# Row layout of the k and q loads, 64x64 transposes, and new orders at the start and the end of a block-sparse attention + soft MoE kernel

## The chip, the core and the metric

The kernel runs on one core of a Trainium2 chip. The metric is the device time of one execution in microseconds (us). Five engines work side by side, each through its own instructions in order: TensorE (PE in the profile, PEld for its weight loads), VectorE (DVE), ScalarE (ACT), GpSimd (POOL) and SyncE (SP, which here only issues DMAs). Matmul results land in PSUM, everything else on the chip lives in SBUF; both have 128 partitions.

## The reference

Four batches (B) of eight heads (H), 768 positions (S), head size 64 (D). In each head the keys are cut into 24 chunks of 32 positions. Of each chunk the minimum and the maximum of k give an upper bound of the score for each query; the six chunks with the highest bound (among the causal ones) are kept, and a causal softmax attention runs over them:

```python
ub = sum(max(q * k_min, q * k_max), axis=-1)         # [q, 24], -1e9 where not causal
top_chunks = argsort(ub)[..., -6:]
scores = where(chunk in top_chunks and causal, q @ k.T / 8, -1e9)
x = softmax(scores) @ v                               # [3072, 512] over all heads
logits = x @ phi                                      # [3072, 32]: 8 experts x 4 slots
d = softmax(logits, axis=0);  slot_input = d.T @ x
slot_out[e] = relu(slot_input[e] @ w1[e]) @ w2[e]
out = softmax(logits, axis=1) @ slot_out
```

## The kernel before, in words

**Pairs.** Work goes in 16 pairs of heads, four pairs to a batch, the two heads of a pair on partitions 0-63 and 64-127. Per pair i:

- `load` (L163) brings k and q from HBM by a POOL-issued DMA, cast to bf16 on the way, two pairs to a DMA from pair 2 on. Partition p holds, of each head, the six rows 6p to 6p+5: for a pair two pieces of 384 numbers. Pair 0 goes another way: two SP DMAs in f32 (L184), then `cast` (L589) to bf16, one head on DVE (L591) and one on ACT (L592).
- `transposes` (L232) makes kT and qT: 12 matmuls (L240), six row groups g times two heads h. Each takes 128 partitions x 64 columns as weights against the 128-column identity and writes 64 partitions x 128 columns: `ps[h*64:(h+1)*64, g, :]`. All of a pair's k (or q) lies in one PSUM tile. `evac_T` (L246, L250) copies it to SBUF, on ACT, and puts the columns into the order of the positions.
- `kmin`, `kmax` (L259, L265, DVE), `heads` (L271, bd), `qneg`, `qpos` (L279, L289; qpos of pair 0 on ACT, L287) prepare the bound; `ubound` (L292) is its matmuls (L299, L309); `select` (L315) takes the eight largest of each row (L320) and makes a mask (L322 on POOL, L323 on DVE), which `ns_transposes` (L331) and `evac_ns` (L339) turn.
- `scores` (L342): per group of blocks, matmuls of q and k (L349) and of the mask (L359), each pair of them on the two halves of the partitions. `expo` (L373, ACT) is the exponential, `mask` (L383, POOL) the causal cut, `pv` (L397) the product with v, `normalise` (L409, L410), `x_transposes` (L419), `evac_x` (L430).

Two PSUM tiles hold scores (pool `p_sc`), two hold everything that is transposed or small (`p_tp`), one holds the products with v (`p_at`).

**MoE.** After each batch: logits (L442), a running maximum, exponentials, `moe_dispatch` (L529; L537 the slot inputs, L541 `zt`, the sums). Weights w1, w2 come by POOL DMAs (L150, L160) spread over the whole kernel; all POOL DMAs run in one queue, one after another.

**Order.** Nothing reorders instructions: each engine does them as the program issues them. A head written out by hand (L594 to L670) does pairs 0 and 1 up to their selections, all scores of pair 0 and the preparation of pair 2; `warm` (L227) issues matmuls whose results nobody reads. From pair 1 on, strings (PLAIN, LOGITS, SLOTS, AFTER, BEFORE_LAST, FINAL; L731 to L736) give the order, and `step` and `final` carry out their words: sc, ex, mk, pv for scores, expo, mask and pv; trk, trq, evk, evq for transposes and their copies of pair i+2; ub, sel, ns, evns for the bound of pair i+1. In FINAL, `pl`, `nl`, `xl`, `el`/`ela` are pv, normalise, transposes and copies (DVE/ACT) of the last pair, three spans of rows each; `lgt` and `lgl` the logits of the last batch without and with the last pair's columns; `pma` the maximum over the first five row blocks of them, joined at L866 with the sixth; `cs` 18 small matmuls (L821) that sum the combine weights of the first three batches, `inv` their reciprocal (L813).

**Tail.** After FINAL: the softmax of the last batch's logits (L866 to L902), `moe_dispatch` of the last batch, two expert layers (L934, L975, L1001, L1011) and the output, by halves of the columns and then whole (L1045, L1031, L1034, L1075), written by SP.

Of the kernel before, what the change touches and what calls it, by code (L numbers as in the profile page):

```python
# [9 lines left out]
F32 = mybir.dt.float32  # L10
# [6 lines left out]
NEG = -1e9  # L17
# [42 lines left out]
def kernel(  # L60
# [75 lines left out]
    for nm in ("k", "q"):  # L136
        ring[nm] = [inp.tile([P, 4, NQT * D], BF16, name=f"{nm}_in{x}") for x in range(2)]
    for x, nm in enumerate(("k", "q")):
        spare = w_sb[EARLY - 4][:, x * 4 * NQT * D:(x + 1) * 4 * NQT * D]
        ring[nm].append(spare.rearrange("p (h c) -> p h c", h=4))  # L140
# [21 lines left out]

    def load(i, nm, n=1):  # L163

        b, j = divmod(i, NPB)
        t = ring[nm][i // 2 % 3][:, 2 * (i % 2):2 * (i % 2 + n)]
        src = {"k": k, "q": q}[nm][b, 2 * j:2 * (j + n)]
        nc.gpsimd.dma_start(out=t, in_=src.rearrange("h (p g) d -> p h (g d)", p=P))
        for x in range(n):
            st[nm, i + x] = t[:, 2 * x:2 * x + 2]  # L170
# [11 lines left out]
    stage = [w_sb[x].bitcast(F32).rearrange("p (h c) -> p h c", c=512)[:, :2, :NQT * D] for x in range(EARLY - 2, EARLY)]  # L182
    for t, src in zip(stage, (k, q)):
        nc.sync.dma_start(out=t, in_=src[0, :2].rearrange("h (p g) d -> p h (g d)", p=P))  # L184
# [47 lines left out]
    def transposes(i, nm, runs=((0, NQT),), home=(p_tp, "tp")):  # L232

        src = st.pop((nm, i))
        st[nm + "ps", i] = []
        for g0, g1 in runs:
            ps = home[0].tile([P, g1 - g0, P], BF16, name="tr_ps", tag=home[1])
            for g in range(g0, g1):
                for h in range(2):
                    nc.tensor.matmul(  # L240
                        ps[h * 64:(h + 1) * 64, g - g0, :], lhsT=src[:, h, g * D:(g + 1) * D], rhs=ident,
                        is_transpose=True,
                    )
            st[nm + "ps", i].append((g0, g1, ps))

    def evac_T(i, nm, *copies):  # L246

        t = tp3.tile([P, S], BF16, name=nm + "T", tag=nm + "T")
        for (g0, g1, ps), copy in zip(st.pop((nm + "ps", i)), copies or (nc.scalar.copy,)):
            copy(  # L250
                t.rearrange("d (p g) -> d p g", g=NQT)[:, :, g0:g1],
                ps.rearrange("d g p -> d p g"),
            )
        st[nm + "T", i] = t
# [334 lines left out]
    def cast(n, nm):  # L589
        st[nm, 0] = ring[nm][0][:, :2]  # L590
        nc.vector.tensor_copy(st[nm, 0][:, 0], stage[n][:, 0])  # L591
# [15 lines left out]
    qneg(0)
    qpos(0)
    nc.vector.tensor_tensor(schunk[:, :, :, 0], squad[:, :, 0, :], squad[:, :, 1, :], op=ALU.add)
    spread_mask(0, NJ, nc.gpsimd.tensor_copy)  # L610
    warm(10)
    ubound(0)
    spread_mask(NJ, NQT, nc.scalar.copy)
    select(0)
    transposes(1, "k", ((0, NQT),), (p_sc, "sc"))
    evac_T(1, "k")
    transposes(1, "q", ((0, NQT),), (p_sc, "sc"))
    evac_T(1, "q")
    load_v(1)
    load(4, "q", 2)  # L620
    warm(3)
    ns_transposes(0)
    evac_ns(0)
    kmin(1)
    kmax(1)
    heads(1)
    qneg(1)
    qpos(1)
    for g in range(5):
        scores(0, g)  # L630
        expo(0, g, g < 4)
        if g == 1:
            load(6, "k", 2)
            warm(3)
        if g == 2:
            warm(1)
    load(6, "q", 2)
    ubound(1)
    select(1)
    load_v(2)  # L640
    load_w(1)
    mask(0, 4)
    transposes(2, "k")
    evac_T(2, "k")
    nc.gpsimd.dma_start(out=phi_sb, in_=moe_phi.rearrange("(hg p) s -> p hg s", p=P))
    scores(0, 5)
    warm(3)
    expo(0, 5)
# [18 lines left out]
    nc.vector.memset(pm_pad, 0.0)
# [68 lines left out]
    FINAL = """sc:1 sc:0 norm sc:2 ex:1 pv:0 pv:2 pv:3 pv:4 mk:1 ctc pv:5 pv:1 ex:0 ex:2 sc:3 xt mk:0 ex:3 norm1 sc:4 mk:2 ex:4 xt1 mk:3 evx pl:0 evx1 sc:5 mk:4 pl:2 pl:1 nl:0 pl:3 nl:1 xl:0 pl:4 lgt el:0 mz lh:2 ex:5 pl:5 lh:3 xl:1 cs nl:2 lgl:0 xl:2 ela:1 lgl:1 ela:2 pma lgl:2 inv"""  # L736
# [40 lines left out]
    def final(what):  # L777
# [20 lines left out]
        elif name == "lgt":  # L798
            st["lgt"] = p_at.tile([P, 2, 512], F32, name="lgt_ps", tag="at")
            st["lg12"] = st["lgt"][:, 0, :2 * NQT * NS].rearrange("p (t o s) -> p t o s", t=NQT, o=2)  # L800
            moe_logits(BL, range(NDG - 1), st["lg12"])
        elif name == "lgl":
            moe_logits(BL, range(NDG - 1, NDG), st["lg12"], range(*SPANS[n]))
        elif name == "pma":
            nc.vector.tensor_reduce(
                pm_a, st["lg12"][:, :NQT - 1, 0, :].rearrange("p t s -> p s t"), axis=AX.X, op=ALU.max)
# [18 lines left out]
    pm_a = small.tile([P, NS], F32, name="pm_a", tag="pm_a")  # L825
# [39 lines left out]
    pm = small.tile([P, NS], F32, name="pm", tag="pm")  # L865
    nc.vector.tensor_tensor(pm, pm_a, lg1[:, NQT - 1], op=ALU.max)  # L866
# [152 lines left out]
    relu(0)  # L1019
    experts_in(1, 0)  # L1020
# [93 lines left out]
```

## Time and profile before

| | |
|---|---|
| median of 3 runs | 157.98 us (157.34 to 158.03) |
| the profiled execution | 157.53 us, of which the span from first to last instruction is 155.8 us |
| granted TensorE clock, mean | 0.987 |

| engine | busy in the span |
|---|---|
| PE | 138.0 us, 89% |
| DVE | 122.4 us, 79% |
| ACT | 122.4 us, 79% |
| POOL | 95.3 us, 61% |

A line of the timeline or of the groups reads: start, duration (both us), engine, line of the kernel, operation, tile written <- tiles read, shape; xN puts N instructions together, and the duration is then from the first start to the last end. In brackets stands how long the engine sat idle before it and what ended that.

### The profile page before, as it was taken

How to read it: one execution, taken by the hardware profiler on the slowest of the kernel's cores; microseconds unless marked ns; L12 is line 12 of the kernel's file. 1: busy time of each engine (PE TensorE's matmuls, PEld its weight loads, DVE VectorE, ACT ScalarE, POOL GpSimd, SP SyncE). 2: the span in 40 equal slices, each digit the busy share in tenths (PEclk: the TensorE clock that was granted, in tenths of full speed). 3: DMA queues.
4: the chain of work that ended last, by engine and by line, in shares of the span. 5: the costliest groups of instructions: out<-in, count | busy, mean ns of one | idle time of the engine just before them, and what ended most of it. 6: DMA issues, size and time to landing. Idle time of an engine off the chain costs nothing.

```text
span 155.8 us, 6087 instructions
## 1 busy us (share of the span) xinstructions
PE 138.0 (89%) x2515; PEld 90.9 (58%) x2515; DVE 122.4 (79%) x450; ACT 122.4 (79%) x167; POOL 95.3 (61%) x196
## 2 busy tenths in 40 slices
PE   7998979999999999999999999999989899776700
PEld 2443546767667676757766776766758745553200
DVE  4777889889898999999999999999775660459800
ACT  3678899999999899999989999998887333437700
POOL 6966992984878769476946947496593990000000
PEclk9999999999999999999999999999999999999995
DMA  4999999999999999999999999999999999989996
GB/s 149 211 183 215 195 196 196 214 178 197 211 217 188 195 214 184 197 207 219 192 196 203 203 207 196 199 194 215 204 210 210 209 195 198 133 271 346 375 403 230
DMA packets 46171, 33.31 MB, mean 214 GB/s; under 512 B 26304, under 2 KB 41664, under 8 KB 46144
## 3 DMA queue, kind: packets, MB, share of 16 engines
q0 software_dynamic: 41328, 25.86, 114.1%
q1 hardware_dynamic: 4816, 7.08, 12.8%
q8 instruction: 19, 0.31, 0.7%
q14 instruction: 8, 0.07, 0.1%
HBM read 52.49 MB, written 6.29 MB: 377 GB/s over the span
## 4 chain that ended last, share of the span: by engine, by line
PE 47%; DVE 23%; ACT 12%; issue 5%; POOL 4%; DMA 2%; DVEq 0%; SPq 0%; ACTq 0%; POOLq 0%
PE sc_ps L349 9%; PE at_ps L397 9%; ACT e_sb L373 8%; PE sc_ps L359 6%; PE tr_ps L240 4%; PE xT_ps L419 3%; DVE mx L320 3%; DMA w_sb<-in_q_dram 2%; PE h_ps L934 2%; DVE mm L259 2%; DVE mm L265 2%; PE ub_ps L299 2%; ACT o_sb L1031 2%; POOL e_sb L383 2%; DVE o_sb L1034 2%
## 5 line engine op out<-in xcount | busy, mean ns | idle before, releaser
L373 ACT ACTIVATE e_sb<-sc_ps 128x768 bf16<-128x768 f32 (+2 forms) x96 | 83.1, 927 | 5.5 <-PE sc_ps L359 4.6
L383 POOL TENSOR_SCALAR_AFFINE_SELECT e_sb<-e_sb 128x256 bf16<-128x256 bf16 x96 | 37.7, 413 | 21.2 <-ACT e_sb L373 20.8
L349 PE MATMUL sc_ps<-qT,kT 64*128 64x384 bf16 (+3 forms) x260 | 37.7, 306 | 1.4 <-ACT e_sb L373 1.3
L359 PE MATMUL sc_ps<-nsT,smask 64*128 64x384 bf16 (+2 forms) x296 | 37.6, 284 | 0.1
L397 PE MATMUL at_ps<-v_t,e_sb 128*128 128x65 bf16 x630 | 26.3, 193 | 0.2
L397 PEld LDWEIGHTS <-e_sb 128*128 128x128 bf16 x630 | 22.4, 97 | 5.2 <-issue 2.8
L320 DVE MAX8 mx<-ub_ps 128x8 f32<-128x8 f32 (+1 forms) x192 | 16.8, 163 | 5.6 <-PE ub_ps L309 3.6
L349 PEld LDWEIGHTS <-kT 64*128 64x128 bf16 x260 | 13.0, 93 | 8.4 <-issue 2.2
L174 POOL DMA_DIRECT2D v_t<-in_v_dram x16 | 16.6, 1041 | 0.5 <-PE sc_ps L359 0.5
L359 PEld LDWEIGHTS <-smask 64*128 64x128 bf16 x296 | 14.8, 95 | 3.5 <-issue 0.6
L410 DVE TENSOR_TENSOR x_sb<-at_ps,inv 128x768 bf16<-128x768 f32 (+3 forms) x18 | 15.6, 868 | 0.6
L259 DVE TENSOR_REDUCE mm<-kT 128x24 bf16<-128x768 bf16 x16 | 15.1, 943 | 0.1
L265 DVE TENSOR_REDUCE mm<-kT 128x24 bf16<-128x768 bf16 x16 | 15.1, 943 | 0.0
L250 ACT COPY qT<-tr_ps 128x768 bf16<-128x768 bf16 x16 | 13.1, 816 | 1.4 <-PE tr_ps L240 1.4
L250 ACT COPY kT<-tr_ps 128x768 bf16<-128x768 bf16 (+1 forms) x16 | 12.7, 796 | 0.1
L230 PE MATMUL warm_ps<-ones_sq 128*128 128x512 bf16 x29 | 9.2, 451 | 1.1 <-DVE ones_sq L180 1.1
L150 POOL DMA_DIRECT2D w_sb<-in_moe_w_dram x14 | 10.0, 715 | 0.0
L299 PEld LDWEIGHTS <-qpn 128*128 128x128 bf16 x192 | 6.0, 96 | 6.2 <-issue 3.6
L430 DVE COPY xT_sb<-xT_ps 128x768 bf16<-128x768 bf16 (+1 forms) x16 | 8.6, 536 | 1.2 <-PE xT_ps L419 1.2
L299 PE MATMUL ub_ps<-bd,qpn 128*128 128x48 bf16 x192 | 7.8, 184 | 1.0 <-DVE qpn L279 0.9
L419 PE MATMUL xT_ps<-ident,x_sb 128*128 128x128 bf16 x96 | 8.4, 220 | 0.0
L323 DVE TENSOR_TENSOR ns_t<-ub_ps,mx 128x288 bf16<-128x288 f32 x16 | 7.3, 457 | 0.5
(170 smaller groups left out, 220.5 us busy)
## 6 DMA issues: line engine op xcount, KB each, us to landing
w_sb<-in_moe_w_dram POOLq DMA_DIRECT2D x14, 1024.0 KB, 16.8
out_dram<-o_sb SPq DMA_DIRECT2D x14, 256.0 KB, 2.9
v_t<-in_v_dram POOLq DMA_DIRECT2D x16, 192.0 KB, 13.8
out_dram<-o_sb SPq DMA_DIRECT2D x5, 512.0 KB, 4.5
w_half<-in_moe_w_dram POOLq DMA_DIRECT2D x8, 256.0 KB, 9.5
k_in<-in_k_dram POOLq DMA_DIRECT2D x5, 384.0 KB, 11.2
q_in<-in_q_dram POOLq DMA_DIRECT2D x5, 384.0 KB, 11.9
w_sb<-in_k_dram POOLq DMA_DIRECT2D x2, 384.0 KB, 10.8
```

Of the source, the lines that this page charges most:

```text
L174: nc.gpsimd.dma_start(out=v_t[i % NV][:, :, :, :D], in_=v[b, 2 * j:2 * j + 2].rearrange("h (g p) d -> p h g d", p=P),)
L250: copy(t.rearrange("d (p g) -> d p g", g=NQT)[:, :, g0:g1], ps.rearrange("d g p -> d p g"),)
L259: nc.vector.tensor_reduce(mm[:, 0, 0, :], kT, axis=AX.X, op=ALU.min)
L265: nc.vector.tensor_reduce(mm[:, 1, 0, :], kT, axis=AX.X, op=ALU.max)
L299: nc.tensor.matmul(o, lhsT=qpn[:, x, t * P:(t + 1) * P], rhs=bd[:, x], start=(t == 0 and x == 0), stop=False,)
L320: nc.vector.max(mx[:, a, :], ub[:, a, :max(8, 4 * t + 4)])
L349: nc.tensor.matmul(ps[:, h, c:c + w], lhsT=kT[r, kg * P:(kg + 1) * P], rhs=qT[r, qs], start=True, stop=False,)
L359: nc.tensor.matmul(ps[:, h, c + (f - t0) * P:c + (l - t0) * P], lhsT=smask[r, x, kg].rearrange("p a b -> p (a b)"), rhs=nsT[r, (f - x * NJ ...
L373: nc.scalar.activation(e[:, :, :w], st.pop(("scps", i, g))[:, :, :w], func=ACT.Exp, scale=scale)
L383: nc.gpsimd.affine_select(out=e[:, :, c:c + P], in_=e[:, :, c:c + P], compare_op=ALU.is_ge, fill=0.0, base=0, pattern=[[0, 2], [1, P]], ch ...
L397: nc.tensor.matmul(o, lhsT=st["e", i, g][:, h, c:c + P], rhs=v_t[i % NV][:, h, kg, :D + 1], start=(kg == 0), stop=(kg == t),)
L410: nc.vector.tensor_tensor(st["x", b][:, t0:t1, 2 * j:2 * j + 2, :].rearrange("p t h d -> p h t d"), at[:, :, :, :D], inv.broadcast_to([P, ...
```

## The change

Three parts.

1. **Layout and transposes.** Partition p now holds 12 consecutive rows of one head (partitions 0-63 the first head of the pair, 64-127 the second): one piece of 768 numbers instead of two of 384. A transpose takes a quarter of the array: 64 partitions x 64 columns of weights against a 64-column identity, to 64 partitions x 64 columns. There are 24 of them for one k or q instead of 12, in the order g, then h. The casts of pair 0 are split by columns (row groups 0-5 and 6-11), no longer by head.
2. **Head.** The hand-written lines become a string HEAD and `head()`, with another order: among others, on ACT the copy of kT comes before the cast of q; on DVE `qneg` of pair 0 comes before `bd`; the transposes of pair 1 stand partly before the bound of pair 0; the bound of pair 1 (ub:1) stands after the fourth group of scores, not after the fifth; `sc:5` and the q transposes of pair 2 come earlier and `ex:5` later; two memsets (pm_pad, pm_lo) move from pair 2's preparation to the start; the first weight load is issued after `spreadp`.
3. **End.** The logits of the last batch without the last pair's columns are cut in two (`lgt:0`, `lgt:1`) and come after the last products with v (`pl:5`); `cs` comes after the last logits; the last copy of xT goes from ACT to DVE; one maximum over all six row blocks replaces the two steps; the reciprocal of the sums comes after the first `relu`; in the last dispatch `zt` comes before the slot inputs.

The orders PLAIN to BEFORE_LAST, and so the work of pairs 1 to 14 but for the transposes' form, are unchanged.

```diff
-        ring[nm] = [inp.tile([P, 4, NQT * D], BF16, name=f"{nm}_in{x}") for x in range(2)]
+        ring[nm] = [inp.tile([P, 2, S], BF16, name=f"{nm}_in{x}") for x in range(2)]
...
+    def head_pairs(t, b, j, n):
+        src = t[b, 2 * j]
+        return bass.AP(src.tensor, src.offset, [[S, P], [P * S, n], [1, S]])
+
     def load(i, nm, n=1):
         b, j = divmod(i, NPB)
-        t = ring[nm][i // 2 % 3][:, 2 * (i % 2):2 * (i % 2 + n)]
-        src = {"k": k, "q": q}[nm][b, 2 * j:2 * (j + n)]
-        nc.gpsimd.dma_start(out=t, in_=src.rearrange("h (p g) d -> p h (g d)", p=P))
+        t = ring[nm][i // 2 % 3][:, i % 2:i % 2 + n]
+        nc.gpsimd.dma_start(out=t, in_=head_pairs({"k": k, "q": q}[nm], b, j, n))
...
-        nc.sync.dma_start(out=t, in_=src[0, :2].rearrange("h (p g) d -> p h (g d)", p=P))
+        nc.sync.dma_start(out=t, in_=head_pairs(src, 0, 0, 1))
...
+    nc.vector.memset(pm_pad, 0.0)
+    nc.vector.memset(pm_lo, 0.0)
...
-    def transposes(i, nm, runs=((0, NQT),), home=(p_tp, "tp")):
+    NG, HP = 12, 64
+    def transposes(i, nm, runs=((0, NG),), home=(p_tp, "tp")):
...
-            ps = home[0].tile([P, g1 - g0, P], BF16, name="tr_ps", tag=home[1])
+            ps = home[0].tile([P, g1 - g0, HP], BF16, name="tr_ps", tag=home[1])
             for g in range(g0, g1):
                 for h in range(2):
+                    r = slice(h * HP, (h + 1) * HP)
                     nc.tensor.matmul(
-                        ps[h * 64:(h + 1) * 64, g - g0, :], lhsT=src[:, h, g * D:(g + 1) * D], rhs=ident,
-                        is_transpose=True,
+                        ps[r, g - g0, :], lhsT=src[r, g * D:(g + 1) * D], rhs=ident[r, r], is_transpose=True,
                     )
...
-    def cast(n, nm):
-        st[nm, 0] = ring[nm][0][:, :2]
-        nc.vector.tensor_copy(st[nm, 0][:, 0], stage[n][:, 0])
-        nc.scalar.copy(st[nm, 0][:, 1], stage[n][:, 1])
+    def cast(n, nm, h, copy):
+        st[nm, 0] = ring[nm][0][:, 0]
+        c = slice(h * S // 2, (h + 1) * S // 2)
+        copy(st[nm, 0][:, c], stage[n][:, 0, c])
...
+    HEAD = """w:6 w:1 ka kd lv:0 caus qd qgrp trk:0 w:1 evk:0 qa trq:0 kmin:0 w:4 kmax:0 w:1 evq:0 lk:4 qsn:0 bd:0 squad schunk w:1 trk:1:s qsp:0 ub:0 w:1 spreada w:2 spreadp lw evk:1 w:1 sel:0 w:1 trq:1:s evq:1 ns:0 evns:0 sc:0 kmin:1 lv:1 kmax:1 lq:4 sc:1 lk:6 w:2 w:1 qsp:1 qsn:1 ex:0 sc:2 mk:0 w:1 ex:1 sc:3 ex:2 mk:2 bd:1 trk:2 ub:1 ex:3 mk:1 sel:1 sc:4 sc:5 evk:2 lq:6 kmin:2 mk:3 ex:4 trq:2 w:1 mk:4 once lv:2 ns:1 w:1 evns:1 w:1 evq:2 lw w:1 kmax:2 phi identf bd:2 qsn:2 ex:5 qsp:2"""
...
-    FINAL = """sc:1 sc:0 norm sc:2 ex:1 pv:0 pv:2 pv:3 pv:4 mk:1 ctc pv:5 pv:1 ex:0 ex:2 sc:3 xt mk:0 ex:3 norm1 sc:4 mk:2 ex:4 xt1 mk:3 evx pl:0 evx1 sc:5 mk:4 pl:2 pl:1 nl:0 pl:3 nl:1 xl:0 pl:4 lgt el:0 mz lh:2 ex:5 pl:5 lh:3 xl:1 cs nl:2 lgl:0 xl:2 ela:1 lgl:1 ela:2 pma lgl:2 inv"""
+    FINAL = """sc:1 sc:0 norm sc:2 ex:1 pv:0 pv:2 pv:3 pv:4 mk:1 ctc pv:5 pv:1 ex:0 ex:2 sc:3 xt mk:0 ex:3 norm1 sc:4 mk:2 ex:4 xt1 mk:3 evx pl:0 evx1 sc:5 mk:4 pl:2 pl:1 nl:0 pl:3 nl:1 xl:0 pl:4 el:0 mz lh:2 ex:5 pl:5 lh:3 lgt:0 xl:1 lgt:1 nl:2 lgl:0 xl:2 ela:1 lgl:1 el:2 lgl:2 pma cs"""
...
+        if b == B - 1:
+            nc.tensor.matmul(zt, lhsT=ones_sq, rhs=d_sb, start=True, stop=True)
         for dg in range(NDG):
...
-        nc.tensor.matmul(zt, lhsT=ones_sq, rhs=d_sb, start=True, stop=True)
+        if b < B - 1:
+            nc.tensor.matmul(zt, lhsT=ones_sq, rhs=d_sb, start=True, stop=True)
...
-                pm_a, st["lg12"][:, :NQT - 1, 0, :].rearrange("p t s -> p s t"), axis=AX.X, op=ALU.max)
+                pm, st["lg12"][:, :, 0, :].rearrange("p t s -> p s t"), axis=AX.X, op=ALU.max)
...
-    nc.vector.tensor_tensor(pm, pm_a, lg1[:, NQT - 1], op=ALU.max)
...
     relu(0)
+    nc.vector.reciprocal(inv_a, st["csa"])
```

More of the change, by code (lines that the diff above doesn't have):

```diff
@@ L181 @@
     nc.vector.memset(ident, 0.0)
-    stage = [w_sb[x].bitcast(F32).rearrange("p (h c) -> p h c", c=512)[:, :2, :NQT * D] for x in range(EARLY - 2, EARLY)]
+    stage = [w_sb[x].bitcast(F32).rearrange("p (i c) -> p i c", i=2)[:, :1, :S] for x in range(EARLY - 2, EARLY)]
     for t, src in zip(stage, (k, q)):
-        nc.sync.dma_start(out=t, in_=src[0, :2].rearrange("h (p g) d -> p h (g d)", p=P))
+        nc.sync.dma_start(out=t, in_=head_pairs(src, 0, 0, 1))
     load(1, "k")
@@ L607 @@
[L607 to L648, printed above, removed]
@@ new lines @@
+    LW = [0, 1]
+    EVAC = {"evk": "k", "evq": "q"}
+    CASTS = {"kd": (0, "k", 0, nc.vector.tensor_copy), "ka": (0, "k", 1, nc.scalar.copy),
+             "qp": (1, "q", 0, nc.gpsimd.tensor_copy), "qd": (1, "q", 0, nc.vector.tensor_copy),
+             "qa": (1, "q", 1, nc.scalar.copy)}
+    DO = {"kmin": kmin, "kmax": kmax, "bd": heads, "qsn": qneg, "qsp": qpos, "ub": ubound,
+          "bdp": lambda i: heads(i, nc.gpsimd),
+          "sel": select, "ns": ns_transposes, "evns": evac_ns, "lv": load_v}
@@ new lines, with head @@
+    HEAD = """w:6 w:1 ka kd lv:0 caus qd qgrp trk:0 w:1 evk:0 qa trq:0 kmin:0 w:4 kmax:0 w:1 evq:0 lk:4 qsn:0 bd:0 squad schunk w:1 trk:1:s qsp:0 ub:0 w:1 spreada w:2 spreadp lw evk:1 w:1 sel:0 w:1 trq:1:s evq:1 ns:0 evns:0 sc:0 kmin:1 lv:1 kmax:1 lq:4 sc:1 lk:6 w:2 w:1 qsp:1 qsn:1 ex:0 sc:2 mk:0 w:1 ex:1 sc:3 ex:2 mk:2 bd:1 trk:2 ub:1 ex:3 mk:1 sel:1 sc:4 sc:5 evk:2 lq:6 kmin:2 mk:3 ex:4 trq:2 w:1 mk:4 once lv:2 ns:1 w:1 evns:1 w:1 evq:2 lw w:1 kmax:2 phi identf bd:2 qsn:2 ex:5 qsp:2"""
+    def head(what):
+        name, *arg = what.split(":")
+        if setup(name):
+            return
+        if name in CASTS:
+            cast(*CASTS[name])
+            return
+        i = int(arg[0])
+        if name == "w":
+            warm(i)
+        elif name in ("trk", "trq"):
+            runs = ((0, NG // 2), (NG // 2, NG)) if what == "trk:0" else ((0, NG),)
+            transposes(i, name[2], runs, (p_sc, "sc") if what == "trk:0" or arg[1:] else (p_tp, "tp"))
+        elif name in EVAC:
+            evac_T(i, EVAC[name], *((nc.scalar.copy, nc.vector.tensor_copy) if what == "evk:0" else ()))
+        elif name in DO:
+            DO[name](i)
+        elif name in ("lk", "lq"):
+            load(i, name[1], 2)
+        elif name == "sc":
+            scores(0, i)
+        elif name == "ex":
+            expo(0, i, False)
+        elif name == "mk":
+            mask(0, i)
@@ L672, in step @@
+    for what in HEAD.split():
+        head(what)
     def step(i, what):
@@ L824 @@
     inv_a = small.tile([P, BL * NQT], F32, name="inv_a", tag="inv_a")
-    pm_a = small.tile([P, NS], F32, name="pm_a", tag="pm_a")
+    pm = small.tile([P, NS], F32, name="pm", tag="pm")
     for i in range(1, NPAIR):
```

114 lines of the change are left out of this document (53 added, 61 removed).

## The prediction

> **What bounds the kernel now.** I read the windows first (which engine is full in which stage), then the chain of work that ended last, then the timeline at the start and the end. One window from the middle, its columns PE, PEld, DVE, ACT, POOL, clock, DMA share, GB/s; and the chain's shares by line:
>
> ```profile
> 24.00:36.74 12.74, 12.74 (x252) 8.77 (x249) 11.64 (x45) 12.63 (x17) 9.43 (x20) 1.00 1.48 197
> by line: PE sc_ps L349 8.6%; PE at_ps L397 8.6%; ACT e_sb L373 8.0%; PE sc_ps L359 6.0%; issue 4.7%; PE tr_ps L240 4.3%; PE xT_ps L419 3.3%; DVE mx L320 2.7%; DMA w_sb<-in_q_dram 2.4%; PE h_ps L934 2.4%; DVE mm L259 2.3%; DVE mm L265 2.2%;
> ```
>
> Two pairs take 12.74 us, 6.37 each; PE is busy for all of it, ACT for 12.63. So from pair 1 on, time added to PE's work comes out at the end, and nothing is gained there by sparing DVE or POOL. The transposes (L240) hold 4.3% of the span on the chain: 0.043 x 155.8 = 6.7 us. At the start the work is a chain from engine to engine with idle time in between, and so it is again around the last batch's softmax (from 122 to 127 us). Those two places the new orders touch.
>
> **Part 1: the transposes.** One tile of them, what runs after it, and three prices of matmuls:
>
> ```profile
> 69.84 0.53 PE L240 MATMUL tr_ps<-ident,w_sb 128*64 128x128 bf16 x12
> 70.30 0.51 PE L419 MATMUL xT_ps<-ident,x_sb 128*128 128x128 bf16 x6
> ```
> ```profile
> L240 PE MATMUL tr_ps<-ident,w_sb x96: 216/219/243, 26.3 to 77.2; 128*64 128x128 bf16 x96
> ```
> ```profile
> 121.93 0.69 PE L442 MATMUL lgt_ps<-phi_sb,xT_sb 128*128 128x64 bf16 x18
> ```
>
> A tile takes PE 0.46 us (69.84 to 70.30). One matmul lasts 219 ns, so the twelve start within 0.53 - 0.22 = 0.31 us. The six xT matmuls, also of 128 columns, start within 0.51 - 0.22 = 0.29 us. Twelve in the time of six: the two heads' matmuls run beside each other on the two column halves of the array, one step of two in 0.31 / 5 = 62 ns. After, there are 12 steps of two matmuls of 64 columns. The nearest price for 64 columns is the logits row: 18 matmuls start within 0.69 - 0.19 = 0.50 us, 29.4 ns each (0.19 is the length of its single matmul at 124.22, below). If two quarters still run beside each other, the tile takes 11 x 29.4 + 219 = 542 ns: +0.012 us. On the chain stand 6.7 / 0.46 = 15 of the 32 tiles: **+0.2 us** (all 32: 0.4).
>
> If each quarter waits for the other, it is 23 x 29.4 + 219 = 895 ns, +0.365 us a tile. That is the upper end, +5.5 us on 15 tiles; the lower end is zero, since no row gives 64 columns for less. I take the low value because column halves are seen side by side here, and row halves too: the score matmuls of two heads (14.59 below), two of 384 columns on 64 partitions each, take 0.34 us together, where the six xT matmuls, also 768 columns in all, take 0.51. What no row shows is both at once.
>
> [...]
>
> ```profile
> L250 ACT COPY qT<-tr_ps 128x768 bf16<-128x768 bf16 x16 | 13.1, 816 | 1.4 <-PE tr_ps L240 1.4
> ...
> k_in<-in_k_dram POOLq DMA_DIRECT2D x5, 384.0 KB, 11.2
> ```
>
> The copies out of PSUM keep their size (768 numbers a partition, 816 ns); only the step between the numbers read changes: I take zero. The loads have half as many pieces of twice the size; of their landings only the first two, by SP, are on the chain (2.4%, q's). I count -0.1 us for those in part 2.
>
> **Part 2: the head.** First up to the first exponential:
>
> ```profile
> 3.92 0.36 DVE L591 CAST k_in<-w_sb 128x384 bf16<-128x384 f32 x1 [1.21 <-DMA w_sb<-in_k_dram]
> 4.70 1.06 POOL L174 DMA_DIRECT2D v_t<-in_v_dram  x1
> ...
> 5.13 0.81 DVE L591 CAST q_in<-w_sb 128x384 bf16<-128x384 f32 x1 [0.85 <-DMA w_sb<-in_q_dram]
> ...
> 7.42 0.94 DVE L265 TENSOR_REDUCE mm<-kT 128x24 bf16<-128x768 bf16 x1
> ...
> 8.40 0.26 DVE L271 TENSOR_TENSOR bd<-mm,headsel 128x96 bf16<-128x96 bf16 x1
> 8.57 0.35 DVE L279 TENSOR_SCALAR qpn<-qT 128x768 bf16<-128x768 bf16 x1
> ```
>
> The chain goes q's landing, DVE's cast, DVE's copy of half of kT, kmin, kmax, bd, qneg, PE. It stays DVE's: moving ACT's kT copy ahead of its cast helps only ACT. qneg before bd saves a wait: bd waits for kmax's end (8.36), qneg doesn't need it and fills that gap, so bd ends about 0.1 us before qneg does now. The cast of q took 0.81 where that of k took 0.36; beside it POOL issued v's load. It still will, so I keep 0.81 and take -0.1 for an earlier landing of q (bounds, cast and landing together, 0 and -0.4). The two moved memsets run while DVE waits for k (1.21 us idle): nothing. Sum **-0.2** (0 to -0.5). The transposes of pair 1, now ahead of ub, stand in time that PE fills with warm.
>
> Then pair 1:
>
> ```profile
> 12.44 4.37 ACT L373 ACTIVATE e_sb<-sc_ps 128x1024 bf16<-128x1024 f32 x5 [0.94 <-PE sc_ps L359]
> ...
> 14.59 0.34 PE L359 MATMUL sc_ps<-nsT,smask 64*128 64x384 bf16 x2
> ...
> 15.68 0.47 PE L299 MATMUL ub_ps<-bd,qpn 128*128 128x48 bf16 x12
> ...
> 16.23 1.06 DVE L320 MAX8 mx<-ub_ps 128x8 f32<-128x8 f32 x12 [1.64 <-PE ub_ps L309]
> ...
> 16.70 0.79 ACT L250 COPY kT<-tr_ps 128x768 bf16<-128x768 bf16 x1
> ...
> 17.38 0.83 ACT L373 ACTIVATE e_sb<-sc_ps 128x768 bf16<-128x768 f32 x1
> ...
> 18.55 0.35 DVE L339 COPY nsT<-ns_ps 128x384 bf16<-128x384 bf16 x1
> ```
> ```profile
> 19.44 1.97 ACT L373 ACTIVATE e_sb<-sc_ps 128x1024 bf16<-128x1024 f32 x2
> ...
> 20.17 0.17 DVE L667 MEMSET pm_pad<- 128x128 f32 x1
> ...
> 20.33 0.63 DVE L279 TENSOR_SCALAR qpn<-qT 128x768 bf16<-128x768 bf16 x1
> ...
> 20.88 0.43 DVE L289 TENSOR_SCALAR qpn<-qT 128x768 bf16<-128x768 bf16 x1
> 21.37 0.34 PEld L299 LDWEIGHTS <-qpn 128*128 128x128 bf16 x11 [0.26 <-DVE qpn L289]
> ...
> 22.34 0.81 ACT L373 ACTIVATE e_sb<-sc_ps 128x768 bf16<-128x768 f32 x1 [0.24 <-PE sc_ps L359]
> ```
>
> DVE idles 1.64 us for ub of pair 1, which stands behind the fifth scores, and those behind ACT. After, ub comes behind the fourth (the row at 14.59, ending 14.93) and one tile of transposes (0.46): 15.35 instead of 15.68, **-0.35**. All that follows on DVE (mx, nsT) and so the first exponential of pair 1 is 0.55 earlier: 18.9. ACT can just follow. Neighbours on it overlap by 0.11 (the copy of kT starts at 16.70, the five exponentials end at 16.81), so five exponentials, two copies and ex:5 are 4.37 + 0.79 + 0.82 + 0.83 - 3 x 0.11 = 6.5 us from 12.44 on: 18.9, or 18.7 with the start's gain. On DVE the memsets go from between bd and qneg (-0.15), and qneg and qpos, 0.63 and 0.43 beside POOL's setup work where qneg of pair 0 took 0.35, get part of 0.36 back, since that setup work stands elsewhere: -0.25 (bounds 0 and -0.36). PE waits for qpos until 21.37; from there on it is full. So the stream of pair 1 starts **0.95 us earlier** (0.2 + 0.35 + 0.15 + 0.25), with bounds 0.4 and 1.4. The exponential at 22.34 waits for PE and moves along.
>
> The first weight load is issued later, behind spreadp (some 2 us). POOL's DMAs land some 11 us after their issue (k_in's row) because earlier ones stand before them, so the queue doesn't run dry: nothing. What POOL does next (the mask's cast, v's load) waits for DVE anyway.
>
> **Part 3: the end.**
>
> ```profile
> 121.12 0.81 ACT L373 ACTIVATE e_sb<-sc_ps 128x768 bf16<-128x768 f32 x1 [0.27 <-PE sc_ps L359]
> ```
> ```profile
> 122.40 0.35 DVE L430 COPY xT_sb<-xT_ps 128x384 bf16<-128x384 bf16 x1
> ...
> 122.45 0.35 PE L759 MATMUL at_ps<-v_t,e_sb 128*128 128x65 bf16 x6
> ...
> 122.83 0.17 DVE L409 RECIPROCAL inv<-at_ps 128x2 f32<-128x2 f32 x1
> 122.91 0.59 PE L821 MATMUL h_ps<-live,cT_all 128*128 128x1 bf16 x18
> ...
> 123.53 0.22 PE L419 MATMUL xT_ps<-ident,x_sb 128*128 128x128 bf16 x1
> ...
> 123.78 0.27 ACT L430 COPY xT_sb<-xT_ps 128x128 bf16<-128x128 bf16 x1 [0.30 <-PE xT_ps L419]
> ...
> 124.22 0.19 PE L442 MATMUL lgt_ps<-phi_sb,xT_sb 128*128 128x64 bf16 x1 [0.41 <-DVE pm_a L805]
> ...
> 124.44 0.19 DVE L866 TENSOR_TENSOR pm<-pm_a,lgt_ps 128x32 f32<-128x32 f32 x1
> 124.55 0.35 DVE L868 TENSOR_REDUCE rm<-lgt_ps 128x6 f32<-128x192 f32 x1
> ```
>
> pl:5 (122.45) can start when its exponential ends, 121.93; then the reciprocal waits only for the copy before it, until 122.75: -0.08. Without cs in front, PE is free for xl:2 as soon as x is there: -0.1 more. The copy on DVE costs 0.2 (between 0.35 for three times the columns and ACT's 0.27): -0.07. The matmul at 124.22 no longer waits for pm_a: -0.1. One maximum over six blocks is as long as rm's row, 0.35, in place of 0.19: +0.16. cs (0.59) runs beside that maximum and may stick out by 0.1. Sum **-0.2** (0 to -0.4). The rest of the tail hangs on this chain and moves with it.
>
> **Sum**, against the profiled execution's 157.53 us (span 155.8 and 1.7 around it): -0.95 - 0.2 + 0.2 = -0.95, so **156.6 us**. The median of the runs is 0.45 above that execution; the same difference from it would give 157.0. A measurement of this kernel can tell about 0.5% (0.8 us) from no change.
>
> **Rivals.** *(2) The gain is given back.* The last weights come late:
>
> ```profile
> L160 POOL DMA_DIRECT2D w_half<-in_moe_w_dram x2: 740/741/742, 127.4 to 128.1; - x2
> ...
> DMA to landing us min/median/max: 9.4/9.8/10.1
> ```
> ```profile
> 138.63 0.39 PE L1011 MATMUL so_last<-w_half,hT_pad 128*32 128x256 bf16 x8
> ```
>
> Issued at 128.1, landed between 137.5 and 138.2, used at 138.63: 0.4 to 1.1 us to spare. If the queue doesn't move, a gain beyond that is lost there; or ACT's fullness takes part of the head's. For it: ACT's limit of 18.7, hardly before 18.9; against: larger pieces may shorten the queue. With 0.6 lost of the 0.95: 157.2 us.
>
> *(3) The quarters don't run beside each other*, the other side. Place: L240, 15 tiles on the chain, up to 26 where PE is full. Price 0.365 each: 157.53 - 1.15 + 5.5 = 161.9, up to 165.9. Partly (45 ns a step: 0.71 us a tile, +0.18): 159.1. It decides from 1.15 / 15 = 0.077 us a tile, a step of 36 ns instead of 29.4. For it: no row shows two quarters at once; against: each halving alone is seen. [...]
>
> **Chances.** Forecast 0.55 (own range 155.8 to 157.4); (2) 0.17; (3) partly 0.09, fully 0.19. Some of the forecast's own range, 0.05, ends within 0.5%: faster 0.50, same 0.22, slower 0.28. From 155.8 to 160.0 lie the forecast, (2) and the part of (3), 0.81.
>
> **What would show it.** A transposes tile of 0.54 us right, 0.7 to 0.9 wrong; ub of pair 1 near 15.1 and its first exponential near 18.9; the bound's matmuls of pair 2 near 20.4; the pair's period still 6.4; the step from the last copy of xT to the maximum's end shorter by 0.2. I am wrong if DVE's q cast grows, if PE waits for w_half, or if the period passes 6.6.

## The result: 3.6% slower

| | before | changed kernel |
|---|---|---|
| median | 158.00 us (157.34 to 158.24, 4 runs) | 163.45 us (163.19 to 163.78, 3 runs) |
| ratio to before | 1 | 1.036 (95% interval 1.032 to 1.039) |
| a profiled execution | 157.53 us, span 155.8 | 162.84 us, span 161.1, clock 0.987 |

A fourth run of the changed kernel was slow (166.86 us, clock 0.972) and is left out, as slow runs are in every ratio below, and the lines of "after" come from the execution of 162.84 us.

**The transposes are as cheap as forecast.** The timeline of PE, after, in the columns of the prediction's rows:

```profile
66.23 0.56 PE L231 MATMUL tr_ps<-ident,q_in 64*64 64x64 bf16 x24
66.73 0.34 PE L339 MATMUL sc_ps<-qT,kT 64*128 64x384 bf16 x2
```

From 66.23 to the next matmul at 66.73 the tile takes PE 0.50 us, where it took 0.46. Twenty-four quarters start within 0.56 - 0.19 = 0.37 us (one lasts 0.19 to 0.20 us), 31 ns for each step of two; in the trace the two of a step start 3 ns apart. They run side by side.

**The head gains more than forecast.** The timeline of the start, after:

```profile
11.89 3.35 ACT L363 ACTIVATE e_sb<-sc_ps 128x1024 bf16<-128x1024 f32 x4 [0.52 <-PE sc_ps L349]
...
14.81 0.47 PE L289 MATMUL ub_ps<-bd,qpn 128*128 128x48 bf16 x12
...
18.61 2.06 ACT L363 ACTIVATE e_sb<-sc_ps 128x1024 bf16<-128x1024 f32 x2 [0.28 <-PE sc_ps L349]
...
19.54 0.69 PE L289 MATMUL ub_ps<-bd,qpn 128*128 128x48 bf16 x12
```

First exponential 11.89 (12.44 before), bound of pair 1 14.81 (15.68), first exponential of pair 1 18.61 (19.44), bound of pair 2 19.54 (before, its first matmul at 21.02 and the rest from 21.38). So the loss comes later. The windows of the middle, first before and then after (length, then PE, PEld, DVE, ACT, POOL busy with instructions started, clock, DMA share, GB/s):

```profile
48.00:60.00 12.00, 11.81 (x254) 8.70 (x250) 11.66 (x43) 11.58 (x16) 9.21 (x18) 1.00 1.44 196
60.00:72.00 12.00, 11.85 (x237) 8.20 (x233) 11.69 (x43) 11.53 (x16) 8.96 (x20) 1.00 1.43 200
```
```profile
36.00:48.00 12.00, 11.68 (x256) 7.92 (x252) 10.44 (x44) 11.76 (x15) 8.31 (x17) 1.00 1.23 209
48.00:60.00 12.00, 10.78 (x259) 7.97 (x256) 10.90 (x36) 10.19 (x15) 7.56 (x17) 1.00 1.41 199
60.00:72.00 12.00, 10.45 (x242) 7.16 (x238) 9.93 (x37) 9.88 (x14) 7.44 (x17) 1.00 1.36 202
```

At full clock (1.00 in these rows) PE has gone from 11.8 busy of 12 to between 10.5 and 10.8 from 48 us on, and with it ACT and DVE: nobody is full any more. What PE waits for stands in the waits of PE, after (engine, tile, line <- releaser: total us, times, longest), and at one place in the timeline:

```profile
PE at_ps L387 <- issue: 1.9, 2, 1.0
...
PE lg_ps L432 <- issue: 0.7, 1, 0.7
PE sc_ps L349 <- issue: 0.7, 2, 0.5
PE ub_ps L299 <- issue: 0.5, 1, 0.5
```
```profile
63.17 0.77 PE L387 MATMUL at_ps<-v_t,e_sb 128*128 128x65 bf16 x20
...
64.89 0.42 PE L387 MATMUL at_ps<-v_t,e_sb 128*128 128x65 bf16 x8 [0.96 <-issue]
```

"issue" means that nothing in the profile released it. Among 28 matmuls of one kind, on data that had long been there, PE stops for 0.96 us. The waits of before have no row of a matmul with "issue" (its weight loads have some, of up to 0.8 us, that run beside matmuls). And the places lie at a fixed distance. In these windows of after, each cut is laid into one of the longer pauses (51.59 to 52.49, 63.94 to 64.89, 70.56 to 71.05, 82.69 to 83.35, 89.09 to 89.55):

```profile
52.30:64.60 12.30, 11.02 (x256) 7.80 (x256) 11.27 (x47) 10.63 (x14) 8.12 (x17) 1.00 1.39 200
64.60:70.90 6.30, 5.67 (x127) 3.92 (x128) 4.80 (x9) 4.78 (x6) 2.74 (x8) 1.00 1.35 208
70.90:83.20 12.30, 11.55 (x256) 8.08 (x255) 10.39 (x41) 11.51 (x15) 8.44 (x18) 1.00 1.35 200
83.20:89.40 6.20, 5.62 (x128) 3.89 (x128) 5.61 (x26) 5.02 (x8) 3.11 (x9) 1.00 1.35 203
```

Matmuls and weight loads together: 512, 255, 511, 256. The profile's page has a queue in pieces of that size, here before and then after (packets, MB, share):

```profile
q8 instruction: 19, 0.31, 0.7%
```
```profile
q8 instruction: 22, 0.36, 0.8%
```

Its packets are 16 KB each (0.36 MB / 22); at 256 rows to a packet that is 64 bytes an instruction. PE's rows went from 5030 to 5793, and three packets were added (763 / 256). So a packet looks like one block of 256 of PE's instructions. Before, no matmul is held up where a block ends; after, several are.

The records of that queue in the trace of after, laid beside PE's rows (us):

| block's first instruction | packet starts | landed | next block's first instruction |
|---|---|---|---|
| 52.49 | 56.29 (+3.79) | 57.18 | 58.69 |
| 58.69 | 62.61 (+3.92) | 63.56 | 64.89, after a pause |
| 64.89 | 68.61 (+3.72) | 69.55 | 71.06, after a pause |
| 76.98 | 81.01 (+4.03) | 81.99 | 83.36, after a pause |
| 83.36 | 87.18 (+3.81) | 88.15 | 89.55, after a pause |

Four us wait, one us transfer, 1.3 to 1.5 us until PE goes on: some 6.2 us a block, beside a DMA share of 1.35 to 1.39 in the windows above. In 6.37 us, PE's time for a pair, that is room for about 263 instructions, an estimate from these five blocks. Before, a pair has 251 (501 in the prediction's window of two pairs); after, 48 more, 299. Before, the packets start 2.4 to 4.2 us after the block's first instruction and land 1.4 to 3.3 us ahead of their use; why they start later in after isn't shown. That was theory A. The rivals: B, the new orders collide with something; C, the quarters cost PE time in themselves; D, the clock.

### The profile page after: what moved, and what is told of

Its sections match the earlier page's. It is cut to its first block, busy times and chain, and to the rows that moved or that the text cites. A ratio compares the mean times of both kernels' runs of the same rounds, so it can differ in the third digit from the quotient of the medians.

```text
span 165.2 us, 6851 instructions
## 1 busy us (share of the span) xinstructions
PE 141.5 (86%) x2896; PEld 94.6 (57%) x2897; DVE 123.8 (75%) x450; ACT 123.1 (75%) x166; POOL 94.7 (57%) x196
## 3 DMA queue, kind: packets, MB, share of 16 engines
q1 hardware_dynamic: 4560, 7.08, 11.8%
HBM read 52.49 MB, written 6.29 MB: 356 GB/s over the span
## 4 chain that ended last, share of the span: by engine, by line
PE 53%; DMA 11%; DVE 11%; issue 7%; ACT 6%; POOL 6%; DVEq 0%; SPq 0%; ACTq 0%; POOLq 0%
PE sc_ps L339 10%; PE at_ps L387 9%; DMA w_sb<-in_moe_w_dram 9%; PE sc_ps L349 7%; PE tr_ps L231 5%; ACT e_sb L363 4%; PE xT_ps L409 4%; PE h_ps L934 2%; POOL e_sb L373 2%; DMA w_sb<-in_q_dram 2%; PE ub_ps L289 2%; PE ns_ps L321 2%; ACT o_sb L1032 2%; DVE o_sb L1035 2%; DVE x_sb L400 2%
## 5 line engine op out<-in xcount | busy, mean ns | idle before, releaser
L339 PE MATMUL sc_ps<-qT,kT 64*128 64x384 bf16 (+3 forms) x260 | 38.2, 308 | 1.5 <-ACT e_sb L363 0.7
L349 PE MATMUL sc_ps<-nsT,smask 64*128 64x384 bf16 (+2 forms) x296 | 38.2, 286 | 0.8 <-issue 0.7
L387 PE MATMUL at_ps<-v_t,e_sb 128*128 128x65 bf16 x630 | 26.9, 195 | 2.3 <-issue 2.1
L249 DVE TENSOR_REDUCE mm<-kT 128x24 bf16<-128x768 bf16 x16 | 15.1, 943 | 0.1
L255 DVE TENSOR_REDUCE mm<-kT 128x24 bf16<-128x768 bf16 x16 | 15.1, 943 | 0.0
L420 DVE COPY xT_sb<-xT_ps 128x768 bf16<-128x768 bf16 (+2 forms) x17 | 8.8, 519 | 3.0 <-PE xT_ps L409 3.0
L312 POOL CAST ns_t<-mx 128x12 bf16<-128x12 f32 x16 | 4.0, 249 | 7.3 <-DVE mx L310 7.3
```

The lines of the kernel that those rows point to most:

```text
L249: nc.vector.tensor_reduce(mm[:, 0, 0, :], kT, axis=AX.X, op=ALU.min)
L339: nc.tensor.matmul(ps[:, h, c:c + w], lhsT=kT[r, kg * P:(kg + 1) * P], rhs=qT[r, qs], start=True, stop=False,)
L349: nc.tensor.matmul(ps[:, h, c + (f - t0) * P:c + (l - t0) * P], lhsT=smask[r, x, kg].rearrange("p a b -> p (a b)"), rhs=nsT[r, (f - x * NJ ...
L387: nc.tensor.matmul(o, lhsT=st["e", i, g][:, h, c:c + P], rhs=v_t[i % NV][:, h, kg, :D + 1], start=(kg == 0), stop=(kg == t),)
```

## The experiments

**The changed kernel again** (no edit).

> The changed kernel unaltered, for a second profile. Theory A (instruction supply): PE's instructions arrive in blocks of 256 (16 KB, the profile's queue 'instruction'), one block on its way while the one before runs, and beside a full DMA a block takes about 6.2 to 6.6 us from the start of the block before it to its first use; 299 instructions a pair then need more than 6.37 us. It expects 163.2 to 163.8 us and PE pauses of 0.4 to 1.2 us with no releaser ('issue'), always 255 to 257 or 511 to 513 PE rows apart, from about 50 us on, each 1.3 to 1.5 us behind the landing of a block. Rival D (granted clock): the pauses go when the clock is near 0.98 all along.

Measured 162.65 us (162.46 and 162.84), a little under A's span; the ratio to before is 1.030 (1.025 to 1.036). This is the profile read above: the pauses labelled "issue" start at 45.9 us with one of 0.30 us, 255 rows before that at 51.6, at a clock of 0.987, which ends D. One pause of 0.62 us, 190 rows after its neighbour, has a releaser of its own (DVE's qpn).

**Part 1 alone, and parts 2 and 3 alone.** `layout_only` is the kernel before with the diff's hunks of ring, `load`, `transposes`, `evac_T` and `cast`; `orders_only` is the changed kernel with those hunks undone:

```diff
-                        ps[r, g - g0, :], lhsT=src[r, g * D:(g + 1) * D], rhs=ident[r, r], is_transpose=True,
+                        ps[h * 64:(h + 1) * 64, g - g0, :], lhsT=src[:, h, g * D:(g + 1) * D], rhs=ident,
+                        is_transpose=True,
```

> The kernel before with part 1 alone (layout and quarter transposes), its head and its end as they were. Theory A (instruction supply): the pauses come from the 48 added PE instructions a pair, so they stay: 162.5 to 165.0 us. Rival B (the new orders are to blame: what runs earlier in the head collides with something later): no pauses, 157.8 to 158.4 us. [...]

> The changed kernel with the old layout and the old twelve transposes: parts 2 and 3 alone. Theory A (instruction supply): as many PE instructions as before, so no pauses, and the head's and the end's gain is seen whole: 158.0 less 1.1 to 1.9 = 156.1 to 156.9 us. Rival B (the new orders are to blame): 162 to 164 us.

`layout_only`: 166.1 us (165.4 to 167.3), 1.053 (1.047 to 1.058), above A's upper bound of 165; its tiles take 0.50 us of PE, as in after, and its "issue" pauses lie 254 to 256 or 511 to 512 rows apart, which a price of the quarters on PE would not explain. `orders_only`: 156.6 us (156.2 to 157.6, 11 runs), 0.993 (0.990 to 0.996). B falls: the orders are the gain, part 1 is all of the loss. `orders_only` beats both kernels, the one before by 0.7%. Part 1 costs 8.3 us with the old orders and 6.0 with the new (162.65 less 156.64). The pauses begin at 24 us there and at 46 here, and in the blocks that begin between 22 and 43 us the packets start 4.5 to 5.0 us after the first instruction there, 3.3 to 3.9 here; why they do isn't explained.

**The same count of instructions without quarters.** The kernel before, each transpose cut into two of 32 weight columns:

```diff
-                    nc.tensor.matmul(
-                        ps[h * 64:(h + 1) * 64, g - g0, :], lhsT=src[:, h, g * D:(g + 1) * D], rhs=ident,
-                        is_transpose=True,
-                    )
+                    for c in range(2):
+                        r = h * 64 + c * 32
+                        nc.tensor.matmul(
+                            ps[r:r + 32, g - g0, :], lhsT=src[:, h, g * D + c * 32:g * D + c * 32 + 32],
+                            rhs=ident, is_transpose=True)
```

> The kernel before, its layout and orders kept, each transpose cut in two of 32 columns of weights (128 rows, 128 moving columns): 24 instead of 12 a tile, as many PE instructions as the changed kernel, but no row halves. Theory A (instruction supply): pauses every 256 PE rows from about 50 us, 161 to 165 us. Rival C (the quarters themselves): no pauses; if four column strips run side by side, a tile takes 0.53 to 0.60 us and the time is 157.8 to 159.0; if they take turns, a tile takes 0.8 to 0.9 us and the time rises by 15 x 0.35 = 5 us without pauses between instructions.

166.2 us (165.7 to 166.7), 1.053 (1.049 to 1.057): as slow as part 1 alone, a little above A's 165. Its timeline and two windows cut in pauses:

```profile
69.29 0.52 PE L242 MATMUL tr_ps<-ident,q_in 128*32 128x128 bf16 x24
69.74 0.34 PE L350 MATMUL sc_ps<-qT,kT 64*128 64x384 bf16 x2
```
```profile
55.30:67.40 12.10, 10.82 (x256) 7.34 (x256) 11.22 (x50) 10.53 (x15) 8.45 (x17) 1.00 1.47 197
67.40:73.70 6.30, 5.59 (x127) 3.71 (x128) 4.89 (x10) 4.90 (x7) 2.60 (x7) 1.00 1.12 213
```

This is the run that decides. The tile takes 0.45 us of PE, no more than the 0.46 before; the layout, the orders and the loads are those of before; as far as PE's time goes, only the count of instructions differs, and 8.4 us are lost, in pauses 512 and 255 instructions apart. C falls as the main cause.

**Half the dose.** The same cut for k alone (`range(2 if nm == "k" else 1)`, 64 columns for q): 275 instructions a pair.

> The kernel before with the cut into 32 columns of weights for k alone: 24 more PE instructions a pair (275) where the full cut had 48 (299) and cost 8.3 us. Theory A (instruction supply) has a threshold: the full dose ran at about 6.9 us a pair, 256 instructions in 5.9 us; at that rate 275 instructions take 6.4 us, PE's own time. So 158 to 160.5 us, with few pauses, where the blocks come latest. Rival C (each cut matmul has a fixed price): half of 8.3 us, 161.5 to 162.5.

159.9 us (159.9 to 160.3), 1.014 (1.010 to 1.019). Half the instructions cost 2.2 us, a quarter of 8.4: a threshold, not a price each. Where the blocks come in time, nothing is lost at all: POOL issues v's load at 57.84 in this trace and at 57.84 in that of before (at 61.72 with the full cut). Its trace has four pauses at block ends, of 0.29, 0.83, 0.62 and 0.30 us, 2.0 us in all, and the first of them is at 61.9 us. (The waits of PE put the second down to DVE's qpn, but it comes at a block end like the others.) Windows cut in these pauses:

```profile
62.00:80.60 18.60, 18.02 (x383) 12.59 (x383) 17.60 (x68) 17.69 (x23) 12.45 (x28) 1.00 1.36 202
80.60:93.20 12.60, 11.51 (x256) 7.95 (x256) 11.49 (x46) 11.37 (x16) 9.04 (x20) 1.00 1.38 203
93.20:105.80 12.60, 12.15 (x255) 8.19 (x255) 11.23 (x44) 11.54 (x16) 7.32 (x17) 1.00 1.48 196
```

That is 766, 512 and 510 instructions, close to three, two and two blocks. So the room for 263 a pair is a low estimate: with 275 no block end held PE up by 0.2 us or more before 61.9 us.

**Half the quarters.** The changed kernel; but for k of pair 0, only row groups 0 to 5 are transposed, the other half of k and q is left out, and the copy writes each twice (the text below says from pair 1 on; q of pair 0 is halved too):

```diff
-    def transposes(i, nm, runs=((0, NG),), home=(p_tp, "tp")):
+    def transposes(i, nm, runs=((0, NG // 2),), home=(p_tp, "tp")):
...
+                parts.pop()[2].rearrange("d (o g) p -> d p o g", o=1).broadcast_to([P, HP, 2, NG // 2]))
```

> The changed kernel with quarters, layout and orders kept, but from pair 1 on only row groups 0 to 5 of a pair's k and q are transposed (12 quarters a tile instead of 24) and the copy out of PSUM writes each of them twice; the other half of k and q is left out of the computation. As many PE instructions as before, still in quarters. Theory A (instruction supply): no pauses, 155.0 to 157.2 us (the orders' gain, and 0.2 us less of PE a tile where ACT allows it). Rival C (a fixed price of each quarter): half of the loss stays, 159 to 160.5 us.

155.7 us (155.6 to 155.8), 0.987 (0.984 to 0.990). With 251 instructions a pair the quarters are harmless, as A says. The tiles are also shorter here (0.38 us from first start to last end), so a small price of each quarter would not show in this run alone.

**The same instructions beside a lighter queue.** In both kernels only a quarter of each whole weight tile is loaded, and the experts read that quarter for the rest (w1's lines; w2's are changed in the same way):

```diff
-            src = moe_w1[i].rearrange("(a p x) f -> p a (x f)", p=P, x=2)
+            src = moe_w1[i].rearrange("(a p x) f -> p a (x f)", p=P, x=2)[:, :1, :F]
...
-                    rhs=w_sb[e][:, dg * F + f * 512:dg * F + (f + 1) * 512],
+                    rhs=w_sb[e][:, f * 512:(f + 1) * 512],
```

> The changed kernel, but of each weight tile that is loaded whole only a quarter comes (256 of 1024 KB, 14 tiles), and the experts read that quarter in place of the rest; PE's instructions are the same. Theory A (instruction supply beside a full DMA): blocks come within 3 to 5 us, the pauses go, 155 to 158 us. Rival C (the quarters themselves) and D (the clock): 161.5 to 163.

> The same lighter weights on the kernel before, as the control of light_after. Theory A: no pauses to lose, so 156.0 to 158.0 us (less where the last weights were waited for), 0 to 1.5 us above light_after. Rival C: 3 us or more below light_after.

`light_after`: ten runs from 156.6 to 161.6 us, median 159.1, at clocks of 0.976 to 0.988, a scatter that no other kernel here has and that isn't explained. The ratio, 1.000 (0.996 to 1.004), is that of the lower five (median 157.9); the clocks of the upper five are hardly lower, so that choice flatters A. `light_before`: 157.2, ratio 0.997 (0.995 to 1.000). So lighter loads are worth 0.3% to before and, by the lower five, 2.9% to after (1.030 to 1.000), with PE's instructions unchanged. By the median of all ten (159.1) after gains 3.6 us, or 2.2%, and A's bound of 158 was too low, C's 161.5 still too high. Windows of `light_after`, and its one long pause:

```profile
48.00:60.00 12.00, 11.85 (x303) 8.99 (x300) 11.65 (x40) 11.38 (x16) 9.22 (x20) 1.00 0.91 108
60.00:72.00 12.00, 11.95 (x272) 8.50 (x269) 11.44 (x43) 11.64 (x16) 8.21 (x18) 1.00 0.97 110
```
```profile
PE sc_ps L349 <- issue: 1.0, 1, 1.0
PE at_ps L387 <- issue: 0.2, 1, 0.2
```

In the same 12 us PE now starts 603 instructions where after had 515, and is full: it can take more than it was given. In this trace the block's packet starts 0.25 us after the block's first instruction where the queues have run dry (56.84 to 57.09; from 56.0 to 56.84 the DMA share is 0.07 and less). Between 22 and 97 us it mostly starts 2.4 to 3.5 us after it (median of all 2.7; in after 3.7), four times 1.1 us or less, and once 4.5 us (78.55 to 83.06). That last one stops PE, from 84.30 to 85.32. Why it waited there is open: the DMA share was 0.59 from 78.55 to 83.06.

**What the orders are worth.** `head_only` is `orders_only` with the old end; `orders_light` is `orders_only` with the lighter weights.

> Part 2 alone: the kernel before with the new head, the old layout, the old transposes and the old end. With both orders 156.64 us were measured against 157.8, and the trace has 1.15 us of gain at 28 to 33 us, 0.7 from 41 us on, about 1.0 behind the last products with v. Theory: the head's 0.7 is passed through whole, 156.9 to 157.3 us. Rival (the last weights' landing takes back every gain, the end's and the head's alike): 157.4 us or more.

> Parts 2 and 3 with the lighter weights (a quarter of each weight tile that is loaded whole; the experts read that quarter in place of the rest). With all weights PE waits 0.29 us for the last piece of w_half, which lands at 137.8 us as before. Theory: with a DMA queue that has room this wait is gone, 155.8 to 156.5 us, 0.8 to 1.4 below the kernel before with the same lighter weights (157.3). Rival (the wait is covered by DVE's and ACT's work on the other half of the output): as with all weights, 156.6 to 157.0.

`head_only`: 157.4 us (156.4 to 158.3, 12 runs), 0.996 (0.992 to 0.999), between the theory's 157.3 and the rival's 157.4, so the median doesn't decide. The granted clock does: eight of the twelve runs have 0.966 to 0.968, four 0.977 to 0.986. At the lower clock `head_only` has 157.6 and before, in the same series, 158.4; at the higher 156.5 and 157.6: a gain of 0.75 to 1.0 us. Its profile is one of the lower clock. The transposes of x run 0.7 us ahead of before at 29 us and 1.30 at 121.50 (122.80 before); the second last layer, at 136.83, is only 0.26 ahead (137.09), without a wait of PE for w_half. Between the two lies this window, before first and then `head_only`:

```profile
124.00:128.00 4.00, 3.48 (x50) 1.89 (x54) 2.61 (x12) 1.29 (x4) 4.00 (x6) 1.00 1.35 194
```
```profile
124.00:128.00 4.00, 4.00 (x49) 1.85 (x52) 1.85 (x9) 1.24 (x3) 3.55 (x6) 0.58 1.36 195
```

PE is busy throughout at a clock of 0.58. So the head's 0.7 us are passed through, and in this trace they are lost where the clock is low, not at the weights.

`orders_light`: 155.9 us (155.6 to 156.7), 0.986 (0.983 to 0.990), 1.3 us below `light_before`, both inside the theory's spans. With all weights, PE's timeline of `orders_only` shows a wait that takes part of the difference, and the same place with the lighter weights goes on without it:

```profile
136.03 1.06 PE L969 MATMUL so_last<-w_sb,hT_pad 128*32 128x256 bf16 x32
...
137.57 0.28 PE L1005 MATMUL so_last<-w_half,hT_pad 128*32 128x256 bf16 x4
138.14 0.29 PE L1005 MATMUL so_last<-w_half,hT_pad 128*32 128x256 bf16 x4 [0.29 <-DMA w_half<-in_moe_w_dram]
139.02 0.61 PE L1040 MATMUL oh_ps<-so_all,cT_all 128*128 128x256 bf16 x4 [0.59 <-DVE so_all L1060]
```

The second last layer starts at 136.03 (137.09 in before's timeline: 1.06 us ahead), the output at 139.02 (139.62: 0.60). The last piece of w_half landed at 138.10, as before (138.19): the queue didn't move. In `orders_light` it landed at 135.07.

## Why the prediction was wrong

The forecast was 156.6 us, from 155.8 to 160.0; it became 163.45. Where the gain went is best seen at POOL's DMA issues (start in us; `split_32` has the old orders):

| POOL's issue | before | orders_only | after | split_32 |
|---|---|---|---|---|
| v_t | 29.61 | 28.46 | 28.03 | 29.55 |
| v_t | 42.37 | 41.67 | 41.36 | 44.11 |
| v_t | 57.84 | 57.07 | 58.39 | 61.72 |
| v_t | 69.86 | 69.11 | 71.95 | 75.05 |
| v_t | 95.86 | 95.17 | 101.58 | 105.09 |
| first w_half | 114.44 | 113.42 | 119.95 | 123.63 |

**Part 1 failed**, at the step "On the chain stand 6.7 / 0.46 = 15 of the 32 tiles: +0.2 us": it cost 6.0 us with the new orders and 8.3 with the old. The tile's own price was nearly right: 0.56 us from first start to last end against 542 ns, 0.50 us as a stretch of PE against 0.46 + 0.012. What was wrong is that PE's time for a tile was taken for the whole cost. Each tile also has 12 more matmuls and 12 more weight loads to be fetched, in all 32 tiles and not in 15: 48 a pair, where the supply had room for some 12 to 24 (263 less 251 by the estimate above; the 24 of `split_32_k` cost nothing up to 61.9 us). PE's rows of before held the count (x252 and x249 in the first row quoted) and the profile's page held the queue; neither was read for it. "The pair's period still 6.4" was the sign given, and it failed: between the first and the fifth row of the table, after takes 73.55 us and `orders_only` 66.71, over the same ten pairs: 7.4 and 6.7 us a pair. Their windows over that stretch, after first (the columns as above):

```profile
28.03:101.58 73.55, 68.31 (x1569) 48.39 (x1566) 65.51 (x229) 65.49 (x85) 47.89 (x104) 1.00 1.34 200
```
```profile
28.46:95.17 66.71, 65.87 (x1327) 46.36 (x1326) 63.93 (x229) 64.67 (x84) 48.51 (x104) 1.00 1.38 201
```

Of the 6.84 us, PE is idle for 73.55 - 68.31 - (66.71 - 65.87) = 4.4 and busy for 2.4 more. `light_after` has the same instructions without most pauses, and its PE is busy 66.68 over that work: 0.8 more than `orders_only`, which is the tiles' own price (20 x 0.04). The other 1.6 us are probably the pauses' hidden part: a matmul counts as busy for 0.19 us where the next one can follow after 0.03, so each of the dozen block ends hides some 0.15. That is argued, not shown. The window of `light_after` over the same work:

```profile
28.03:96.31 68.28, 66.68 (x1567) 47.95 (x1566) 63.48 (x229) 64.88 (x85) 47.22 (x103) 1.00 0.99 117
```

**Rival 3 gave the right time for a wrong reason.** Its span, 161.9 to 165.9, holds the result. Its mechanism, quarters that take turns, would have made the tile 0.9 us; it is 0.56 from first start to last end. Both heads' quarters write one PSUM tile, and still a step of two takes 31 ns.

**Part 2 held**, and is best read without part 1, in `orders_only`:

```profile
12.29 3.34 ACT L358 ACTIVATE e_sb<-sc_ps 128x1024 bf16<-128x1024 f32 x4 [0.56 <-PE sc_ps L344]
...
15.17 0.47 PE L284 MATMUL ub_ps<-bd,qpn 128*128 128x48 bf16 x12
...
18.98 2.02 ACT L358 ACTIVATE e_sb<-sc_ps 128x1024 bf16<-128x1024 f32 x2 [0.28 <-PE sc_ps L344]
...
19.88 0.72 PE L284 MATMUL ub_ps<-bd,qpn 128*128 128x48 bf16 x12
```

15.17 against "near 15.1", 18.98 against 18.9; the bound of pair 2 at 19.88 is earlier than 20.4. The 0.95 us were 0.7 on PE, inside the bounds of 0.4 and 1.4. They stay 0.7 to 1.0 up to 104 us; POOL's first row in the table is 1.15 ahead, since POOL there issues the load earlier beside PE's work. The transposes of x, before and then `orders_only`:

```profile
29.66 0.51 PE L419 MATMUL xT_ps<-ident,x_sb 128*128 128x128 bf16 x6
```
```profile
28.94 0.51 PE L404 MATMUL xT_ps<-ident,x_sb 128*128 128x128 bf16 x6
```

The layout brings the start another 0.3 to 0.4 us (11.89, 14.81, 18.61 in after). Most of it stands on DVE at q's landing, which the prediction put at 0.1; `orders_only` first, then after:

```profile
5.29 0.66 DVE L581 CAST q_in<-w_sb 128x384 bf16<-128x384 f32 x1 [0.98 <-DMA w_sb<-in_q_dram]
```
```profile
4.99 0.59 DVE L587 CAST q_in<-w_sb 128x384 bf16<-128x384 f32 x1 [0.77 <-DMA w_sb<-in_q_dram]
```

**Part 3 held.** From the last exponential to the experts' first matmul of the last batch `orders_only` gains 0.19 us (the exponential 121.12 to 120.14, the matmul 127.46 to 126.29), forecast 0.2. The sign given for it was a bad one: the last copy of xT itself came earlier, and the step from it to the maximum's end is 0.08 longer, not 0.2 shorter.

**Rival 2 came true as well**, in `orders_only`: of 1.06 us, 0.60 are left behind w_half, and 0.7 in the span. Without part 1 the change would have been 156.6 us, the forecast's own number, and that is luck in part: the forecast has part 1's +0.2 in it and nothing for w_half. Parts 2 and 3 had been put at 1.15 us; the medians differ by 1.17 (157.81 and 156.64), the two traces by 0.7.

## What to carry to other kernels

Count the instructions that an engine must fetch, not only the time that they take: where PE is the bound beside a busy DMA (a share of 1.12 to 1.47 in the windows above of after and `split_32`), compare PE's instructions in a stage (the counts of the windows) with what the instruction queue delivers there, 256 in about 6.2 us in after. Where that kept up, added instructions cost no pause (the 24 a pair of `split_32_k` none of 0.2 us or more up to 61.9 us); where it did not, the stage took some 24 ns (6.2 us / 256, an estimate) for every instruction in it, and packing the array more finely, which makes two instructions out of one, lost more than it saved: part 1 cost 6.0 to 8.3 us. Pauses called "issue" at a fixed distance in rows (255 to 256 or 511 to 512 in the windows of after), on data long there, were the mark of it; fewer instructions (`half_quarters`, 155.7 us) and a lighter DMA queue (`light_after`, a share of 0.91 to 0.97 in its windows, 157.9 us as the median of the lower five runs) are the two cures seen here.

## What was not expected of the hardware

- A block of 256 instructions took some 6.2 us in after (5.9 to 6.8 in windows of `split_32`) from the first instruction of the block before it to its own, beside a DMA share of 1.35 to 1.39 in after; in `light_after`, where the queues had run dry (a share of 0.07 and less), the packet started 0.25 us after the first instruction of the block before, against 3.7 to 4.0 in the five blocks of after.
- Quarters of the array and strips of 32 columns run side by side in one PSUM tile: 24 quarters start within 0.37 us in after, 24 strips of 128 moving columns take 0.45 us of PE in `split_32`, as 12 transposes with 64 columns of weights do before (0.46).
- Before, the kernel stood some 12 to 24 instructions a pair (an estimate: 263 and 275 less 251) below the threshold without one matmul that waited for "issue"; only the time of the packets, 1.4 to 3.3 us ahead of their use, shows how near it was.
